# First q projection in four passes of 128 tokens, with wq's rows loaded ahead of x tiles 2 and 3

## Chip, cores and metric

One core of a Trainium2 chip runs the whole program. The metric is the device time of that core in microseconds, the median of several executions. The span in a profile, from the first to the last instruction, is about 1.8 us shorter (1616.3 us in an execution of 1618.12 us). No run here was in the slower state, so no run is left out.

## The reference, cut to what matters

```python
x = x + A(layernorm(x), wqkv, wo)      # dilated local attention, 32 heads of 32, window 8, dilation 2
x = x + B(layernorm(x), w1, w3, w2)    # SwiGLU, 1024 -> 3584 -> 1024
x = x + A(layernorm(x), wqkv, wo)
x = x + B(layernorm(x), w1, w3, w2)
# x: 1 x 2048 x 1024 bf16; wqkv: 1024 x 3072
```

The kernel works in chunks of 512 tokens, each of four tiles of 128. q, k and v are projections on TensorE. Attention itself (products, softmax, weighted sum) is elementwise work on VectorE and gives `oT`, which TensorE multiplies by `wo`.

## The kernel before

The change touches the head, which is the q projection of the first chunk. Its loads are issued in this order on the SP queue:

```python
load_tile(0, 0, 512, nc.sync)          # x tile 0, halves on two queues
load_tile(0, 512, D, nc.scalar)
load_tile(1, 0, D, nc.sync)            # every further piece here is 256 KB
loads(0, 2)                            # rows 0, 1 of wq, one DMA each
load_tile(2, 0, D, nc.sync)
loads(2, 4)
load_tile(3, 0, D, nc.sync)
loads(4, 8)                            # then k's two weight tiles (1 MB each) and x of chunk 1 (1 MB)
```

It computes q in three passes: tile 0 row by row as wq lands, tile 1 block by block, then tiles 2 and 3 together in matmuls of 256 columns. The last pass ends in four stores to DRAM, and between these stores come the loads that are needed next:

```python
for i, acc in enumerate(accumulators(2, 2 * P)):
    for b in range(2):
        for kk in range(KT):
            product(acc[:, b, :], kk, 2 * i + b, tok, kk == 0, kk == KT - 1)
    nc.scalar.copy(hT[:, 2 * i:2 * i + 2, tok], acc[:])
    nc.sync.dma_start(q_rows[:, 2 * i:2 * i + 2, 0:CH], hT[:, 2 * i:2 * i + 2, :])
    then[i]()     # x of chunk 2 | v weights | v weights | x of chunk 3
...
first_q(w_tiles[0:2], load_wq, (lambda: load_x(2), load_weight, load_weight, lambda: load_x(3)))
```

The SP queue works in order: a load written behind a store is issued only when that store's data is ready (in the kernel before, SP waits 10.6 us for the data of the first q store, and x of chunk 2 goes out behind it).

Of the kernel before, what the change touches and what calls it, by code (L numbers as in the profile page):

```python
# [7 lines left out]
FP32 = mybir.dt.float32  # L8
BF16 = mybir.dt.bfloat16
# [6 lines left out]
def kernel(  # L16
# [13 lines left out]
    nc = tc.nc  # L30
    cfg = dict(cfg or {})
    P = 128
    _, S, D = A_x.shape
    F = B_w1.shape[1]
    KT = D // P
    W, DIL, Dh = 8, 2, 32
    assert D == 1024 and KT == 8 and D // Dh == 32
    CH = 512
    NCH = S // CH
    TPC = CH // P  # L40
# [7 lines left out]
    scale = float(Dh) ** -0.5  # L48
    EPS = 1e-5
    BOOST = 3000  # L50
    NWARM = 13
    fsplits = [(0, 16), (16, NF)] if NF > 16 else [(0, NF)]
    HTN = max(b - a for a, b in fsplits)

# [21 lines left out]
    psum = ctx.enter_context(tc.tile_pool(name="psum", bufs=8, space=PSUM))  # L76
# [70 lines left out]
    ident = const.tile([P, P], BF16, name="ident")  # L147
# [13 lines left out]
    hT = const.tile([P, HTN, CH], BF16, name="hT")  # L161
# [3 lines left out]
    def warm(n):  # L165
        for i in range(n):
            pw = bank("pw")
            nc.tensor.matmul(pw[:], lhsT=zero[:, 0, 0:P], rhs=zero[:, 0:2, :].rearrange("p a b -> p (a b)"),
                             start=True, stop=True)
# [8 lines left out]
    KH = KT // 2  # L178
# [51 lines left out]
    def first_q(ws, loads, then):  # L230


        xnT = xnTs["Q", 0, 0] = xtp.tile([P, KT, CH], BF16, name="xnT")
        st = small.tile([P, TPC, 2, 6], FP32, name="st1", bufs=1)
        mv = small.tile([P, TPC, 2], FP32, name="mv1", bufs=1)
        sd = small.tile([P, TPC], FP32, name="sd1", bufs=1)
        rstd = small.tile([P, TPC], FP32, name="rstd1", bufs=1)
        q_rows = qkv_d[0][0][:].rearrange("i t s -> (i t) s").rearrange("(b p) s -> p b s", p=P)

        def load_tile(j, h0, h1, queue):  # L240
            queue.dma_start(x_sb[:, j, h0:h1], xin[:, j, h0:h1])  # L241

        load_tile(0, 0, 512, nc.sync)
        load_tile(0, 512, D, nc.scalar)
        load_tile(1, 0, D, nc.sync)
        loads(0, 2)
        load_tile(2, 0, D, nc.sync)
        loads(2, 4)
        load_tile(3, 0, D, nc.sync)
        loads(4, 8)  # L250
        preload = small.tile([P, 1], FP32, name="preload", bufs=1)
        nc.scalar.activation(preload[:], epst[:], ACTF.Sqrt)

        def stats(j, hh):
            nc.vector.bn_stats(st[:, j, hh, :], x_sb[:, j, hh * 512:(hh + 1) * 512])  # L255

        def deviation(j):
            nc.vector.bn_aggr(mv[:, j, :], st[:, j, :, :])
            nc.scalar.activation(sd[:, j:j + 1], mv[:, j, 1:2], ACTF.Sqrt, bias=epst[:])  # L259

        def apply(j, parts=1):
            nc.vector.reciprocal(rstd[:, j:j + 1], sd[:, j:j + 1])
            xn = xnp.tile([P, D], BF16, name="xn")
            for i in range(parts):
                d = slice(i * D // parts, (i + 1) * D // parts)
                nc.vector.tensor_scalar(xn[:, d], x_sb[:, j, d], mv[:, j, 0:1], rstd[:, j:j + 1],  # L266
                                        op0=ALU.subtract, op1=ALU.mult)
            return xn

        def transpose(xn):  # L270
            pTs = []
            for h in range(2):
                pT = psum.tile([P, KH, P], BF16, name="pT", tag="mm")
                for kk in range(KH):
                    nc.tensor.transpose(pT[:, kk, :], xn[:, (h * KH + kk) * P:(h * KH + kk + 1) * P], ident[:])  # L275
                pTs.append(pT)
            return pTs

        def evacuate(j, h, pTs, copy):
            copy(xnT[:, h * KH:(h + 1) * KH, j * P:(j + 1) * P], pTs[h][:])  # L280

        def product(out, kk, b, tok, start, stop):
            nc.tensor.matmul(out, lhsT=ws[kk // KH][:, kk % KH, b * P:(b + 1) * P], rhs=xnT[:, kk, tok],  # L283
                             start=start, stop=stop, skip_group_check=True)

        def accumulators(per, n):
            return [psum.tile([P, per, n], FP32, name="pq", tag="mm") for _ in range(KT // per)]

        warm(NWARM)
        stats(0, 0)  # L290
        stats(0, 1)
        deviation(0)
        stats(1, 0)
        xn = apply(0, 2)
        pTs = transpose(xn)
        evacuate(0, 0, pTs, nc.scalar.copy)
        stats(1, 1)
        evacuate(0, 1, pTs, nc.vector.tensor_copy)
        deviation(1)

        accs = accumulators(4, P)
        tok = slice(0, P)

        def step0(kk):
            for b in range(KT):
                product(accs[b // 4][:, b % 4, :], kk, b, tok, kk == 0 and b % 4 == 0, kk == KT - 1)

        for kk in range(6):
            step0(kk)
        stats(2, 0)  # L310
        xn = apply(1)
        pTs = transpose(xn)
        for h in range(2):
            evacuate(1, h, pTs, nc.scalar.copy)
        for kk in range(6, KT):
            step0(kk)
        stats(2, 1)
        deviation(2)
        for i in range(2):
            nc.scalar.copy(hT[:, 4 * i:4 * i + 4, tok], accs[i][:])  # L320

        accs = accumulators(4, P)
        tok = slice(P, 2 * P)

        def block1(b):
            for kk in range(KT):
                product(accs[b // 4][:, b % 4, :], kk, b, tok, kk == 0, kk == KT - 1)
            if b % 4 == 3:
                nc.scalar.copy(hT[:, b - 3:b + 1, tok], accs[b // 4][:])

        stats(3, 0)
        xn = apply(2)
        stats(3, 1)
        deviation(3)
        for b in range(3):
            block1(b)
        pTs = transpose(xn)
        for h in range(2):
            evacuate(2, h, pTs, nc.scalar.copy)
        xn = apply(3)  # L340
        for b in range(3, 5):
            block1(b)
        pTs = transpose(xn)
        evacuate(3, 0, pTs, nc.scalar.copy)
        evacuate(3, 1, pTs, nc.vector.tensor_copy)
        for b in range(5, KT):
            block1(b)

        tok = slice(2 * P, CH)
        for i, acc in enumerate(accumulators(2, 2 * P)):  # L350
            for b in range(2):
                for kk in range(KT):
                    product(acc[:, b, :], kk, 2 * i + b, tok, kk == 0, kk == KT - 1)
            nc.scalar.copy(hT[:, 2 * i:2 * i + 2, tok], acc[:])
            nc.sync.dma_start(q_rows[:, 2 * i:2 * i + 2, 0:CH], hT[:, 2 * i:2 * i + 2, :])
            then[i]()
        qkv_at[0, 0, 0] = now["act"] + DMA / 2

    def tree(n, mul, dst):
# [144 lines left out]
    w_tiles, due, used = [], [], [0]  # L504

    def load_weight(pieces=1):

        if len(w_tiles) == len(seq):
            return
        kind, i, n, *rest = seq[len(w_tiles)]  # L510
        if kind == "qkv":
            w = wp.tile([P, KH, D], BF16, name="wqkv", tag="w")
            step = KH // pieces
            for k0 in range(0, KH, step):
                nc.sync.dma_start(w[:, k0:k0 + step, :],
                                  wqkv_v[:, n * KH + k0:n * KH + k0 + step, i * D:(i + 1) * D])
        elif kind == "w2":
            w = wp.tile([P, 8, 512], BF16, name="w2t", tag="w")
            nc.sync.dma_start(w[:, 0:n, :], w2_v[:, i:i + n, rest[0] * 512:(rest[0] + 1) * 512])
        else:  # L520
            w = wp.tile([P, KT, FG * P], BF16, name=kind + "t", tag="w")
            v = w1_v if kind == "w1" else w3_v
            nc.sync.dma_start(w[:, :, 0:n * P], v[:, :, i * P:(i + n) * P])
        w_tiles.append(w)
# [151 lines left out]
    def load_x(c):  # L676
        nc.sync.dma_start(x_sb[:, c * TPC:(c + 1) * TPC, :], xin[:, c * TPC:(c + 1) * TPC, :])
# [3 lines left out]
    def load_wq(k0, k1):  # L681
        for kk in range(k0, k1):
            nc.sync.dma_start(w_tiles[kk // KH][:, kk % KH, :], wqkv_v[:, kk, 0:D])  # L683
        if k1 == KT:
            load_weight()
            load_weight()
            load_x(1)

    first_q(w_tiles[0:2], load_wq, (lambda: load_x(2), load_weight, load_weight, lambda: load_x(3)))
    xnT_at["Q", 0, 0], norm_left["Q", 0, 0] = now["pe"], 0  # L690
    queue_norm(("Q", 0, 1), 1, 0)
    queue_norm(("Q", 0, 1), 1, 1)
# [3 lines left out]
    for c in range(NCH):  # L696
        for which in range(3):
# [4 lines left out]
            then = ()  # L702
            if c == 0 and which == 0:
                continue
            if c == 2 and which == 0:
                then = (None, None, lambda: nc.sync.dma_start(wo[:], wo_v))
            if c == 2 and which == 1:
                then = (load_weight, None, load_weight)
# [50 lines left out]
```

## Time and profile before

| | before |
|---|---|
| median, 6 runs | 1618.99 us (1618.64 to 1619.38) |
| span of the profile | 1616.3 us |
| first k-projection matmul | 24.64 us |
| attention begins on VectorE | 47.74 us |
| last piece of `oT` of the second half chunk written | 160.67 us |

The page of the kernel before: its span, and the chain that ended last by engine, as shares of the span.

```profile
span 1616.3 us, 19263 instructions
...
PE 99%; DMA 0%; SPq 0%; DVE 0%; ACT 0%; issue 0%
```

Followed back from the last instruction, the chain stays on TensorE almost to the start. The waits of TensorE (line, what it waited for, total us, times, longest us):

```profile
PE pw L168 <- DVE psm L163: 1.2, 1, 1.2
PE pq L283 <- DVE st L255: 0.7, 1, 0.7
PE pq L283 <- ACT xnT L280: 0.4, 1, 0.4
PE pT L275 <- DVE xn L266: 0.3, 1, 0.3
```

All four are in the first 16 us. The timeline of TensorE (start us, duration us, engine, line, operation, output from inputs, count, and in brackets the idle time ahead of the group and what ended it):

```profile
10.25 1.30 PE L283 MATMUL pq<-xnT,wqkv 128*128 128x128 bf16 x16 [0.70 <-DVE st L255]
...
15.86 0.62 PE L275 MATMUL pT<-ident,xn 128*128 128x128 bf16 x8 [0.29 <-DVE xn L266]
...
24.64 114.12 PE L591 MATMUL ps<-xnT,wqkv 128*128 128x512 bf16 x528
...
159.32 3.62 PE L552 MATMUL po<-wo,oT 128*128 128x512 bf16 x16
162.78 3.62 PE L591 MATMUL ps<-xnT,wqkv 128*128 128x512 bf16 x16
```

L283 is the q projection, L591 the k and v projections, L552 the output projection by `wo`. A matmul shown alone has 0.39 us, but in a row they start every 0.216 us, so the time of a group is read from one start to the next. TensorE is full from 24.64 us on. The line at 159.32 us reads `oT` of the second half chunk. The timeline of VectorE has the first attention product and the last piece of that `oT`:

```profile
47.74 1.21 DVE L424 TENSOR_TENSOR pr<-qT,kT 128x2048 bf16<-128x2048 bf16 x1
...
160.38 0.29 DVE L371 TENSOR_TENSOR oT<-tm 128x256 bf16<-128x256 bf16 x1
```

The last piece is done at 160.38 + 0.29 = 160.67 us. The matmul that reads it is the eighth of its group, and would start at 159.32 + 7 x 0.216 = 160.83 us. **So TensorE shows no wait there, but it missed one by only 0.16 us.**

The timeline of the SP queue (issue times; "x2" is two issues merged). L355 is a q store, L677 x of chunk 2, L515 v's weights, L217 the DMA transposes and L600 the stores of k:

```profile
20.21 0.37 SPq L355 DMA_DIRECT2D qkv_d<-hT  x1
20.63 0.47 SPq L677 DMA_DIRECT2D x_sb<-in_A_x_dram  x1
21.96 0.37 SPq L355 DMA_DIRECT2D qkv_d<-hT  x1
22.37 1.12 SPq L515 DMA_DIRECT2D wqkv<-in_A_wqkv_dram  x1
...
26.94 10.12 SPq L217 DMA_TRANSPOSE xnT<-xn  x2
37.16 1.04 SPq L600 DMA_DIRECT2D qkv_d<-sgt  x2
```

### The profile page before, as it was taken

The page shows a single profiled execution, that of the slowest core. Times are in us where ns is not written, and L with a number is a line of the kernel's source. Part 1 is how long each engine was busy: PE and PEld are TensorE (multiplying, and loading weights), DVE is VectorE, ACT ScalarE, POOL GpSimd, SP SyncE. Part 2 cuts the span into 40 slices and gives each one's busy share as a digit, 9 for nine tenths or more (in the row PEclk, how much of TensorE's full clock was granted, in tenths as well). Part 3 has the DMA queues.
Part 4 walks back from the last instruction along what each step waited for, and adds up shares of the span by engine and source line. Part 5 has one row for each costly group of instructions (what it writes and reads, how often), then busy time and mean ns, then how long its engine had stood idle before and what let it go on. Part 6 is the DMA issues. An engine that isn't in the chain of part 4 may idle for free.

```text
span 1616.3 us, 19263 instructions
## 1 busy us (share of the span) xinstructions
PE 1610.7 (100%) x7609; PEld 805.3 (50%) x7609; DVE 1176.6 (73%) x1965; ACT 353.6 (22%) x547; POOL 1.9 (0%) x12
## 2 busy tenths in 40 slices
PE   9999999999999999999999999999999999999999
PEld 6666544444445544455444554445544444444444
DVE  5999898989899899998998449983599832222212
ACT  4433311212112230222302123021230212011110
POOL 0000000000000000000000000000000000000000
PEclk9999999999999999999999999999999999999999
DMA  9565855466537773577553776528684266436440
GB/s 314 149 190 158 254 178 169 129 193 190 170 105 236 222 203 125 169 208 249 160 186 120 211 239 175 186 97 259 210 223 158 93 194 170 143 108 218 157 130 27
DMA packets 336427, 285.82 MB, mean 177 GB/s; under 512 B 69712, under 2 KB 318928, under 8 KB 336208
## 3 DMA queue, kind: packets, MB, share of 16 engines
q1 hardware_dynamic: 336192, 284.46, 58.0%
q8 instruction: 59, 0.97, 0.2%
q14 instruction: 32, 0.26, 0.0%
q10 hardware_dynamic: 144, 0.13, 0.0%
HBM read 239.47 MB, written 29.36 MB: 166 GB/s over the span
## 4 chain that ended last, share of the span: by engine, by line
PE 99%; DMA 0%; SPq 0%; DVE 0%; ACT 0%; issue 0%
PE acc L658 24%; PE pu L642 24%; PE pg L634 24%; PE ps L591 20%; PE po L552 7%; PE pq L283 1%; DMA wqkv<-in_A_wqkv_dram 0%; SPq L683 0%; SPq L241 0%; DVE xn L266 0%; ACT xnT L280 0%; PE pT L275 0%; DVE st L255 0%; ACT sd L259 0%; DVE x_sb L668 0%
## 5 line engine op out<-in xcount | busy, mean ns | idle before, releaser
L642 PE MATMUL pu<-xnT,w3t 128*128 128x512 bf16 x1792 | 423.4, 379 | 0.0
L634 PE MATMUL pg<-xnT,w1t 128*128 128x512 bf16 x1792 | 423.4, 379 | 0.0
L658 PE MATMUL acc<-w2t,hT 128*128 128x512 bf16 (+1 forms) x1804 | 389.7, 378 | 0.0
L591 PE MATMUL ps<-xnT,wqkv 128*128 128x512 bf16 x1472 | 319.2, 379 | 0.0
L638 ACT ACTIVATE sg<-pg 128x512 bf16<-128x512 f32 x224 | 133.6, 597 | 773.0 <-PE pg L634 719.4
L646 DVE TENSOR_TENSOR hT<-sg,pu 128x512 bf16<-128x512 bf16 x224 | 152.6, 681 | 186.8 <-PE pu L642 177.8
L658 PEld LDWEIGHTS <-hT 128*128 128x128 bf16 x1804 | 176.5, 98 | 210.5
L642 PEld LDWEIGHTS <-w3t 128*128 128x128 bf16 x1792 | 175.4, 98 | 211.4
L634 PEld LDWEIGHTS <-w1t 128*128 128x128 bf16 x1792 | 175.3, 98 | 211.4
L591 PEld LDWEIGHTS <-wqkv 128*128 128x128 bf16 x1472 | 211.1, 143 | 106.7
L424 DVE TENSOR_TENSOR pr<-qT,kT 128x2048 bf16<-128x2048 bf16 x128 | 156.2, 1221 | 87.2 <-DMA kT<-qkv_d 85.1
L668 DVE TENSOR_TENSOR x_sb<-x_sb,acc 128x512 bf16<-128x512 bf16 x129 | 87.3, 677 | 107.6 <-PE acc L658 107.4
L484 DVE TENSOR_TENSOR tm<-At,vT 128x2048 bf16<-128x2048 bf16 x128 | 156.1, 1220 | 2.4
L595 ACT CAST sgt<-ps 128x512 bf16<-128x512 f32 x184 | 106.7, 585 | 230.7 <-PE ps L591 211.9
L369 DVE TENSOR_TENSOR tm<-tm 128x1024 bf16<-128x1024 bf16 (+1 forms) x256 | 134.5, 550 | 0.4
L369 DVE TENSOR_TENSOR pr<-pr 128x1024 bf16<-128x1024 bf16 (+1 forms) x256 | 134.0, 551 | 0.5
L552 PE MATMUL po<-wo,oT 128*128 128x512 bf16 x512 | 115.7, 379 | 0.0
L552 PEld LDWEIGHTS <-oT 128*128 128x128 bf16 x512 | 50.1, 98 | 60.1 <-DVE oT L371 0.2
L189 DVE BATCH_NORM_STATS2 st<-x_sb 128x6 f32<-128x512 bf16 x120 | 75.9, 671 | 4.6 <-DMA x_sb<-in_A_x_dram 4.6
L557 DVE TENSOR_TENSOR x_sb<-x_sb,po 128x512 bf16<-128x512 bf16 x64 | 43.3, 684 | 19.2 <-PE po L552 18.9
L638 ACT ACT_TABLE_LOAD x31 | 39.8, 1283 | 51.2 <-PE pg L634 51.0
L446 DVE STREAM_TRANSPOSE psmT<-psm 128x2048 bf16<-128x2048 bf16 x16 | 36.9, 2306 | 0.2
(85 smaller groups left out, 402.3 us busy)
## 6 DMA issues: line engine op xcount, KB each, us to landing
w1t<-in_B_w_dram SPq DMA_DIRECT2D x56, 1024.0 KB, 5.5
w3t<-in_B_w_dram SPq DMA_DIRECT2D x56, 1024.0 KB, 8.0
w2t<-in_B_w_dram SPq DMA_DIRECT2D x48, 1024.0 KB, 5.4
wqkv<-in_A_wqkv_dram SPq DMA_DIRECT2D x28, 1024.0 KB, 6.8
qkv_d<-sgt SPq DMA_DIRECT2D x92, 256.0 KB, 2.9
qT<-qkv_d SPq DMA_DIRECT2D x16, 512.0 KB, 8.4
w2t<-in_B_w_dram SPq DMA_DIRECT2D x16, 512.0 KB, 5.2
kT<-qkv_d SPq DMA_DIRECT2D x14, 544.0 KB, 9.5
```

Source lines behind the costliest of these rows:

```text
L369: nc.vector.tensor_tensor(b[:, 0:m, :], b[:, 0:m, :], b[:, m:2 * m, :], op=ALU.add)
L424: V.tensor_tensor(pr[:], qT[:], kT[:, :, k0:k0 + TCH], op=ALU.mult)
L484: V.tensor_tensor(tm[:], At[:], win, op=ALU.mult)
L552: nc.tensor.matmul(ps[:], lhsT=oT[:, t, j * P:(j + 1) * P], rhs=wo[:, t, hh * 512:(hh + 1) * 512], start=(t == 0), stop=(t == KT - 1))
L591: nc.tensor.matmul(ps[:], lhsT=ws[kk // KH][:, kk % KH, t::KT], rhs=xnT[:, kk, :], start=(kk == 0), stop=(kk == KT - 1))
L595: nc.scalar.copy(sgt[:, t - t0, :], ps[:])
L634: nc.tensor.matmul(pg[:], lhsT=w1t[:, kk, fi * P:(fi + 1) * P], rhs=xnT[:, kk, :], start=(kk == 0), stop=(kk == KT - 1))
L638: nc.scalar.activation(sg[:], pg[:], ACTF.Silu)
L642: nc.tensor.matmul(pu[:], lhsT=w3t[:, kk, fi * P:(fi + 1) * P], rhs=xnT[:, kk, :], start=(kk == 0), stop=(kk == KT - 1))
L646: nc.vector.tensor_tensor(hT[:, f - f0, :], sg[:], pu[:], op=ALU.mult)
L658: nc.tensor.matmul(acc[:], lhsT=hT[:, f - f0, j * P:(j + 1) * P], rhs=w2ts[(f - f0) // 8][:, (f - f0) % 8, q0:q0 + step], start=(f == f0), ...
L668: nc.vector.tensor_tensor(xs, xs, acc[:], op=ALU.add)
```

## The change

The intent is a shorter head. wq's rows go ahead of x tiles 2 and 3; the last pass, which needed tiles 2 and 3 together, becomes two passes of 128 tokens, so that tile 3 is needed later; the first copies out of PSUM (the memory into which TensorE writes) are cut finer, so that the first product starts sooner; and x of chunk 2 goes right behind x of chunk 1. With 128-token passes there are two q stores of 512 KB, the first at half of the last pass.

```diff
-    NWARM = 13
+    NWARM = 12
...
-        loads(0, 2)
+        loads(0, 4)
         load_tile(2, 0, D, nc.sync)
-        loads(2, 4)
+        loads(4, 8)
         load_tile(3, 0, D, nc.sync)
-        loads(4, 8)
+        load_weight()
+        load_weight()
+        load_x(1)
+        load_x(2)
...
-        pTs = transpose(xn)
-        evacuate(0, 0, pTs, nc.scalar.copy)
+        p0, p1, p2 = transpose(xn, (0, 2, 4, 8))
+        evacuate(0, p0, nc.scalar.copy)
+        evacuate(0, p1, nc.scalar.copy)
... (pass of tile 1 and 256-column pass of tiles 2 and 3 taken out)
+        for j in range(1, TPC):
+            if j + 1 < TPC:
+                xn = apply(j + 1)
+            if j + 2 < TPC:
+                for hh in range(2):
+                    stats(j + 2, hh)
+                deviation(j + 2)
+            for i, acc in enumerate(accumulators()):
+                for b in range(4):
+                    for kk in range(KT):
+                        product(j, acc[:, b, :], kk, 4 * i + b, kk == 0)
+                    if j + 1 < TPC and (i, b) == (1, 0):
+                        parts = transpose(xn, (0, 4, 8))
+                        for part in parts:
+                            evacuate(j + 1, part, nc.scalar.copy)
+                keep(j, i, acc)
+                if j == TPC - 1:
+                    nc.sync.dma_start(q_rows[:, 4 * i:4 * i + 4, 0:CH], hT[:, 4 * i:4 * i + 4, :])
+                    then[i]()
...
-    first_q(w_tiles[0:2], load_wq, (lambda: load_x(2), load_weight, load_weight, lambda: load_x(3)))
+    def load_v1():
+        load_weight()
+        load_x(3)
+
+    first_q(w_tiles[0:2], load_wq, (load_weight, load_v1))
```

More of the change, by code (lines that the diff above doesn't have):

```diff
@@ L268, in apply, with transpose, evacuate, product @@
             return xn
-        def transpose(xn):
+        def transpose(xn, cuts):
             pTs = []
-            for h in range(2):
-                pT = psum.tile([P, KH, P], BF16, name="pT", tag="mm")
-                for kk in range(KH):
-                    nc.tensor.transpose(pT[:, kk, :], xn[:, (h * KH + kk) * P:(h * KH + kk + 1) * P], ident[:])
-                pTs.append(pT)
-            return pTs
-        def evacuate(j, h, pTs, copy):
-            copy(xnT[:, h * KH:(h + 1) * KH, j * P:(j + 1) * P], pTs[h][:])
-        def product(out, kk, b, tok, start, stop):
-            nc.tensor.matmul(out, lhsT=ws[kk // KH][:, kk % KH, b * P:(b + 1) * P], rhs=xnT[:, kk, tok],
-                             start=start, stop=stop, skip_group_check=True)
-        def accumulators(per, n):
-            return [psum.tile([P, per, n], FP32, name="pq", tag="mm") for _ in range(KT // per)]
+            for k0, k1 in zip(cuts, cuts[1:]):
+                pT = psum.tile([P, k1 - k0, P], BF16, name="pT", tag="mm")
+                for kk in range(k0, k1):
+                    nc.tensor.transpose(pT[:, kk - k0, :], xn[:, kk * P:(kk + 1) * P], ident[:])
+                pTs.append((k0, k1, pT))
+            return pTs
+        def evacuate(j, part, copy):
+            k0, k1, pT = part
+            copy(xnT[:, k0:k1, j * P:(j + 1) * P], pT[:])
+        def product(j, out, kk, b, start):
+            nc.tensor.matmul(out, lhsT=ws[kk // KH][:, kk % KH, b * P:(b + 1) * P],
+                             rhs=xnT[:, kk, j * P:(j + 1) * P], start=start, stop=kk == KT - 1,
+                             skip_group_check=True)
+        def accumulators():
+            return [psum.tile([P, 4, P], FP32, name="pq", tag="mm") for _ in range(2)]
+        def keep(j, i, acc):
+            nc.scalar.copy(hT[:, 4 * i:4 * i + 4, j * P:(j + 1) * P], acc[:])
         warm(NWARM)
@@ L294, in first_q @@
         xn = apply(0, 2)
-        pTs = transpose(xn)
-        evacuate(0, 0, pTs, nc.scalar.copy)
+        p0, p1, p2 = transpose(xn, (0, 2, 4, 8))
+        evacuate(0, p0, nc.scalar.copy)
+        evacuate(0, p1, nc.scalar.copy)
         stats(1, 1)
-        evacuate(0, 1, pTs, nc.vector.tensor_copy)
+        evacuate(0, p2, nc.vector.tensor_copy)
         deviation(1)
-        accs = accumulators(4, P)
-        tok = slice(0, P)
-        def step0(kk):
-            for b in range(KT):
-                product(accs[b // 4][:, b % 4, :], kk, b, tok, kk == 0 and b % 4 == 0, kk == KT - 1)
@@ L308, in first_q @@
-        for kk in range(6):
-            step0(kk)
-        stats(2, 0)
-        xn = apply(1)
-        pTs = transpose(xn)
-        for h in range(2):
-            evacuate(1, h, pTs, nc.scalar.copy)
-        for kk in range(6, KT):
-            step0(kk)
+        xn = apply(1)
+        stats(2, 0)
         stats(2, 1)
         deviation(2)
-        for i in range(2):
-            nc.scalar.copy(hT[:, 4 * i:4 * i + 4, tok], accs[i][:])
-        accs = accumulators(4, P)
-        tok = slice(P, 2 * P)
@@ L325, in block1 @@
-        def block1(b):
-            for kk in range(KT):
-                product(accs[b // 4][:, b % 4, :], kk, b, tok, kk == 0, kk == KT - 1)
-            if b % 4 == 3:
-                nc.scalar.copy(hT[:, b - 3:b + 1, tok], accs[b // 4][:])
-        stats(3, 0)
-        xn = apply(2)
-        stats(3, 1)
-        deviation(3)
-        for b in range(3):
-            block1(b)
-        pTs = transpose(xn)
-        for h in range(2):
-            evacuate(2, h, pTs, nc.scalar.copy)
-        xn = apply(3)
@@ L341, in first_q @@
-        for b in range(3, 5):
-            block1(b)
-        pTs = transpose(xn)
-        evacuate(3, 0, pTs, nc.scalar.copy)
-        evacuate(3, 1, pTs, nc.vector.tensor_copy)
-        for b in range(5, KT):
-            block1(b)
-        tok = slice(2 * P, CH)
-        for i, acc in enumerate(accumulators(2, 2 * P)):
-            for b in range(2):
-                for kk in range(KT):
-                    product(acc[:, b, :], kk, 2 * i + b, tok, kk == 0, kk == KT - 1)
-            nc.scalar.copy(hT[:, 2 * i:2 * i + 2, tok], acc[:])
-            nc.sync.dma_start(q_rows[:, 2 * i:2 * i + 2, 0:CH], hT[:, 2 * i:2 * i + 2, :])
-            then[i]()
+        accs = accumulators()
@@ new lines, in first_q @@
+        for kk in range(KT):
+            for b in range(KT):
+                product(0, accs[b // 4][:, b % 4, :], kk, b, kk == 0 and b % 4 == 0)
+            if kk == 4:
+                parts = transpose(xn, (0, 4, 8))
+                for part in parts:
+                    evacuate(1, part, nc.scalar.copy)
+        for i in range(2):
+            keep(0, i, accs[i])
+        for j in range(1, TPC):
[7 more added lines that the diff above has]
+                for b in range(4):
+                    for kk in range(KT):
+                        product(j, acc[:, b, :], kk, 4 * i + b, kk == 0)
+                    if j + 1 < TPC and (i, b) == (1, 0):
+                        parts = transpose(xn, (0, 4, 8))
+                        for part in parts:
+                            evacuate(j + 1, part, nc.scalar.copy)
[3 more added lines that the diff above has]
+                    then[i]()
@@ L683, in load_wq @@
             nc.sync.dma_start(w_tiles[kk // KH][:, kk % KH, :], wqkv_v[:, kk, 0:D])
-        if k1 == KT:
-            load_weight()
-            load_weight()
-            load_x(1)
-    first_q(w_tiles[0:2], load_wq, (lambda: load_x(2), load_weight, load_weight, lambda: load_x(3)))
+    def load_v1():
+        load_weight()
+        load_x(3)
+    first_q(w_tiles[0:2], load_wq, (load_weight, load_v1))
     xnT_at["Q", 0, 0], norm_left["Q", 0, 0] = now["pe"], 0
```

## The prediction

> **What bounds it now.** The span is 1616.3 us; TensorE is busy 1610.7 us. The list of TensorE's waits has four entries, 2.6 us in all, all in the first 16 us. In the timeline TensorE then runs gap-free from the first k-projection matmul at 24.64 us to its end, 0.216 us per 512-column matmul. So a change of the first q projection is worth exactly how far it moves that 24.64 us.
>
> The head has two limits. (1) Until about 12.2 us it is the arrival of wq's rows: weight loads wait for a DMA before row 3 (8.92 us), row 4 (10.24) and row 5 (10.92). In the table by stretches the DMA engines are full from 7 to 18 us, near 400 GB/s. Each 256 KB piece takes 0.66 us (row 3 to row 4: two pieces, 1.32 us). (2) Then TensorE's own work, with one hole: about 0.46 us before 15.86 us, where the transposes of x tile 3 wait for its normalised rows.
>
> **What the change does.**
> - Loads. The Trainium skill ("DMA: Bandwidth & Descriptors", Queues, rings and completion order) says that an engine consumes descriptors in ring order; the trace's even spacing agrees. Before, row 7 is piece 12 (x0, x1, two rows, x2, two rows, x3, four rows); after, piece 11. Counting from row 3's 8.92 us at 0.66 us each, I estimate rows 0 to 3 at 6.3, 6.9, 7.6, 8.3; x2 8.9; rows 4 to 7 at 9.6, 10.2, 10.9, 11.56; x3 12.2 us. Before, row 7's loads start near 12.24 (40 matmuls begin at 11.78). Gain 0.68 us.
> - The hole before tile 3's transposes: they now come a whole pass later (about 18 us), x3 lands at 12.2, and ScalarE's deviation no longer stands behind it. Gain 0.46 us.
> - 64 matmuls of 256 columns (16.32 to 24.64 us less 24 small ones: 6.95 us, 0.109 each) become 128 of 128 columns at 0.0557 (40 matmuls, 11.83 to 14.06): 7.13 us. Cost 0.18 us. The skill's isolated gap of N/2.4 + 2.5 ns ("TensorE: Matmul & The Clock Gate", Back-to-back issue gap) says 56 and 109 ns, as measured.
> - One warm-up matmul less and the earlier first product (about 7.0 instead of 7.35 us): nothing, since row 7 ends pass 0 in either case.
> - k's weights and x of chunk 1 keep their place; x of chunk 2 fills the DMA dip at 18 to 22 us. q stores become two of 512 KB. No stall for TensorE.
>
> **Sum.** Row 7 at 11.56, its 8 matmuls to 12.0, 192 matmuls at 0.0557 = 10.7, two groups of transposes at 0.45: the k projection starts at 23.6 us instead of 24.64. Everything after moves along unchanged. Gain 1.0 us of 1618.9: predicted 1617.9 us, range 1616.8 to 1619.1. Faster by over 2%: 0.005; within 2%: 0.99; slower: 0.005.
>
> **What would show it.** First k matmul near 23.6 us; row 7's weights near 11.6; weight loads waiting for DMA before most rows of pass 0; no wait between 12 and 24 us; TensorE without gaps later; matmul time of passes 1 to 3 about 3.6 us each.
>
> **What would make it wrong.** ScalarE is tight: tile 1's copies out of PSUM stand behind tile 2's deviation, which waits for x2; they end near 11.9, so a late x2 stalls pass 1. Rows may land later than even spacing says. TensorE waits for rows through pass 0, and if its clock dropped there, 128-column passes would show it. A new gap at the k or v weights would also take back the gain. Run-to-run spread (0.7 us before) is nearly as large as the effect.

## More of the kernel before

```python
# normalised x of later chunks is transposed by DMA, issued from the same SP queue
nc.sync.dma_start_transpose(out=xnT[:, :, j * P:(j + 1) * P], in_=xn[:])
...
# k and v: ScalarE copies the product into one of 3 staging buffers, SP stores it (stg: bufs=3)
nc.scalar.copy(sgt[:, t - t0, :], ps[:])
...
# output projection: TensorE needs oT, which VectorE's attention makes
for t in range(KT):
    nc.tensor.matmul(ps[:], lhsT=oT[:, t, j * P:(j + 1) * P], rhs=wo[:, t, hh * 512:(hh + 1) * 512], ...)
```

The order of each engine's instructions is fixed when the program is built. A projection by `wo` is placed at a point of TensorE's order, and if `oT` isn't there by then, TensorE stands.

## The result, and the profile after

| | before | after |
|---|---|---|
| median, 6 runs each | 1618.99 us | 1619.0 us (1618.81 to 1619.2) |
| span of the profile | 1616.3 us | 1617.2 us |
| first k-projection matmul | 24.64 us | 23.99 us |
| attention begins | 47.74 us | 48.75 us |
| last piece of that `oT` written | 160.67 us | 161.69 us |

The ratio is 1.000 (95% interval 0.9987 to 1.0013). A ratio is the mean time of one kernel's fast runs over that of the other's of the same rounds, so it is not quite the ratio of the medians quoted here. The time did not move, yet the head did become shorter: k starts 0.65 us sooner. The profile shows where that went. The page of the changed kernel:

```profile
span 1617.2 us, 19240 instructions
...
PE 89%; DVE 8%; issue 1%; DMA 1%; ACT 1%; SPq 0%; ACTq 0%; DVEq 0%
```

The chain that ended last no longer stays on TensorE: 8% of it is on VectorE. TensorE's waits in the changed kernel:

```profile
PE po L539 <- DVE oT L358: 1.2, 2, 0.9
PE pw L168 <- DVE psm L163: 1.2, 1, 1.2
PE pq L287 <- DMA wqkv<-in_A_wqkv_dram: 0.5, 1, 0.5
PE pT L278 <- DVE xn L269: 0.3, 1, 0.3
```

There is a new one, `po` (the output projection) waiting for `oT`. In TensorE's timeline (L287 q, L578 k and v, L539 output projection):

```profile
9.89 0.62 PE L287 MATMUL pq<-xnT,wqkv 128*128 128x128 bf16 x8 [0.45 <-DMA wqkv<-in_A_wqkv_dram]
...
23.99 114.13 PE L578 MATMUL ps<-xnT,wqkv 128*128 128x512 bf16 x517
...
158.68 1.46 PE L539 MATMUL po<-wo,oT 128*128 128x512 bf16 x6
161.08 0.39 PE L539 MATMUL po<-wo,oT 128*128 128x512 bf16 x1 [0.95 <-DVE oT L358]
161.75 2.12 PE L539 MATMUL po<-wo,oT 128*128 128x512 bf16 x9 [0.27 <-DVE oT L358]
163.70 3.62 PE L578 MATMUL ps<-xnT,wqkv 128*128 128x512 bf16 x15
```

Up to 158.68 us TensorE is ahead of the kernel before by 0.64 us (158.68 against 159.32). Undisturbed, the 16 matmuls of the group take 3.45 us (159.32 to 162.78). Here 163.70 - 158.68 = 5.02 us pass, a stall of 1.57 us. From there on it is 163.70 against 162.78, that is 0.92 us behind, and it stays so: the spans differ by 0.9 us. So the head gave 0.65 us and one stall took 1.57.

(The spans of the two profiles differ by 0.9 us, but the medians by nothing. One profile is one execution, and k's start scatters from run to run by some 0.4 us, as the table of runs further down shows. In its second profile the unchanged head, in e2_before_v_early, started k at 25.01 us instead of 24.64. That is not the whole 0.9 us: the six timed executions of the kernel before have spans of about 1616.8 to 1617.6, their times less 1.8, and none is as quick as the profiled one.)

VectorE explains the stall. The first attention product and the last piece of that `oT`:

```profile
48.75 1.21 DVE L411 TENSOR_TENSOR pr<-qT,kT 128x2048 bf16<-128x2048 bf16 x1
...
161.40 0.29 DVE L358 TENSOR_TENSOR oT<-tm 128x256 bf16<-128x256 bf16 x1
```

Attention begins 1.01 us later than before, and its `oT` is done 1.02 us later. What holds VectorE until 48.75 us is seen in the chain of waits of the changed kernel between 22 and 50 us (start us, us, what):

```profile
38.19 2.47 DMA qkv_d<-sgt
...
40.76 0.06 ACT sgt L582
...
41.62 0.20 ACT sd L194
...
48.83 1.14 DVE pr L411
```

From the end backwards: VectorE's statistics go in step with ScalarE's square roots (`sd`). ScalarE had to wait before 40.76 us with the copy of k into a staging buffer (`sgt`), because the store that was to free this buffer (`qkv_d<-sgt`) was issued only at 38.19 us. It stood idle for 5.05 us there; in the kernel before for 3.48 us, until 39.76. That store stood on the SP queue behind the two DMA transposes (L217). The SP queue:

```profile
23.01 0.37 SPq L342 DMA_DIRECT2D qkv_d<-hT  x1
23.43 0.51 SPq L502 DMA_DIRECT2D wqkv<-in_A_wqkv_dram  x1
...
27.22 10.87 SPq L217 DMA_TRANSPOSE xnT<-xn  x2
38.19 1.05 SPq L587 DMA_DIRECT2D qkv_d<-sgt  x2
```

L342 is the first q store, L502 v's first weights, L217 the transposes and L587 the stores of k. v's weights were issued at 23.43 and 25.21 us, before at 22.37 and 24.40. x of chunk 3 behind them went out at the same time as before (25.88 and 25.86 us). The stores of k were issued at 38.19 instead of 37.16 us, about the 1.01 us that attention lost. Of these 1.03 us only 0.28 lie in the start of the transposes (27.22 against 26.94); the other 0.75 is that the two transposes held the queue for 10.87 instead of 10.12 us. In the second profile of the changed kernel, e7_after_again, they started at 26.93 us, as before, and held it for 11.68. The table by stretches from 22 to 24 us (columns: busy us of TensorE, its weight loads, VectorE, ScalarE, GpSimd, each with instructions, then the granted TensorE clock, DMA share, GB/s), the kernel before and then the changed one:

```profile
22.00:24.00 2.00, 2.00 (x21) 1.78 (x20) 1.97 (x5) 0.58 (x1) 0.00 (x0) 1.00 0.96 196
...
22.00:24.00 2.00, 2.00 (x40) 2.00 (x38) 1.94 (x4) 0.58 (x1) 0.00 (x0) 1.00 0.18 67
```

In the changed kernel the DMA engines move 67 GB/s there: x of chunk 2 had been loaded early, and nothing else had been let go. (Before, a like gap lay at about 19 to 21 us.)

### The profile page after: what moved, and what is told of

Its sections match the earlier page's. It is cut to its first block, busy times and chain, and to the rows that moved or that the text cites. A ratio compares the mean times of both kernels' runs of the same rounds, so it can differ in the third digit from the quotient of the medians.

```text
span 1617.2 us, 19240 instructions
## 1 busy us (share of the span) xinstructions
PE 1603.3 (99%) x7525; PEld 806.0 (50%) x7672; DVE 1176.4 (73%) x1964; ACT 354.0 (22%) x549; POOL 1.9 (0%) x12
## 4 chain that ended last, share of the span: by engine, by line
PE 89%; DVE 8%; issue 1%; DMA 1%; ACT 1%; SPq 0%; ACTq 0%; DVEq 0%
PE acc L645 24%; PE pg L621 23%; PE pu L629 23%; PE ps L578 12%; PE po L539 6%; DVE pr L411 1%; DVE tm L471 1%; DVE tm L356 1%; DVE pr L356 1%; DVE st L189 1%; PE pq L287 1%; DMA wqkv<-in_A_wqkv_dram 1%; DVE xn L214 0%; DVE At L455 0%; DVE L L435 0%
## 5 line engine op out<-in xcount | busy, mean ns | idle before, releaser
L578 PE MATMUL ps<-xnT,wqkv 128*128 128x512 bf16 x1440 | 317.5, 379 | 1.7
L578 PEld LDWEIGHTS <-wqkv 128*128 128x128 bf16 x1472 | 211.1, 143 | 106.8
L539 PE MATMUL po<-wo,oT 128*128 128x512 bf16 x503 | 115.4, 379 | 1.8 <-DVE oT L358 1.2
L539 PEld LDWEIGHTS <-oT 128*128 128x128 bf16 x512 | 50.0, 98 | 61.7 <-DVE oT L358 2.0
```

The lines of the kernel that those rows point to most:

```text
L578: nc.tensor.matmul(ps[:], lhsT=ws[kk // KH][:, kk % KH, t::KT], rhs=xnT[:, kk, :], start=(kk == 0), stop=(kk == KT - 1))
```

## The experiments

The theory (A): the head's gain is real. It is lost because v's weights and x of chunk 3 are let go only by q stores, and these now come later. So the DMA transposes end later on the queue, the stores of k and then attention come late, and TensorE meets an unfinished `oT`. Rivals: B, the chain on VectorE is set by something else than these loads; C, x of chunk 2 going ahead delays the rest; D, early loads are worth something by themselves. Each experiment is compared with the kernel before on the same chip. All were correct.

The table holds what the argument rests on, in us. "k" is the first k matmul and "att" the first attention product. "late" is the end of the last piece of `oT` less the moment at which TensorE would read it, which is k + 136.19, from before's 160.83 - 24.64. "stall" is what TensorE's timeline shows at that group over 3.45 us.

| run | k | att | late | stall | span | median | before, same chip |
|---|---|---|---|---|---|---|---|
| before | 24.64 | 47.74 | -0.16 | 0 | 1616.3 | 1618.99 | |
| after | 23.99 | 48.75 | 1.51 | 1.57 | 1617.2 | 1619.0 | 1618.99 |
| e1_v_early | 23.76 | 46.04 | -1.01 | 0 | 1615.4 | 1617.11 | 1618.83 |
| e2_before_v_early | 25.01 | 46.27 | -1.76 | 0 | 1616.7 | 1618.01 | 1618.83 |
| e3_dve_1us | 24.83 | 48.61 | 0.48 | 0.56 | 1617.1 | 1619.07 | 1618.83 |
| e4_x2_back | 23.67 | 50.62 | 3.65 | 5.27 | 1620.6 | 1622.59 | 1618.83 |
| e5_rows_only | 23.96 | 47.72 | 0.48 | 0.55 | 1616.2 | 1618.18 | 1618.52 |
| e6_wide_last | 23.74 | 46.73 | -0.27 | 0 | 1615.4 | 1617.04 | 1618.52 |
| e7_after_again | 24.04 | 49.25 | 1.93 | 1.99 | 1617.7 | 1619.23 | 1618.52 |
| e8_early_dve_1us | 23.93 | 47.75 | 0.55 | 0.62 | 1616.2 | 1617.99 | 1618.52 |
| e9_quarter_stores | 23.37 | 47.45 | 0.79 | 0.86 | 1615.9 | 1617.9 | 1618.85 |
| e10_rows_first | 23.87 | 45.83 | -1.31 | 0 | 1615.5 | 1616.71 | 1618.85 |
| e11_v_early_again | 23.92 | 46.11 | -1.11 | 0 | 1615.6 | 1617.37 | 1618.85 |

Two regularities hold in every row. The last piece of `oT` ends 112.9 us after attention begins (112.89 to 112.94; 113.17 in e2_before_v_early, where VectorE also had to wait 0.18 us for TensorE). And the span is k + 1591.66 us (1616.3 - 24.64, from before) + stall, within 0.1 us.

### e1_v_early

```diff
         load_x(2)
+        load_weight()
+        load_weight()
+        load_x(3)
...
-                    then[i]()
```

> The changed kernel with v's two weight tiles and x of chunk 3 issued ahead of the q stores, right behind x of chunk 2. Theory A (the 0.65 us won in the head is lost because the attention chain on VectorE starts 1.01 us late, 48.75 instead of 47.74 us, since v's weights wait on the queue behind the later and larger q stores; TensorE then stalls 1.5 us on oT near 159 us): attention starts well before 47.7 us (estimate 43 to 46), the stall on oT is gone, the k projection still starts at about 24.0 us, and the span is 1.5 us under the changed kernel's 1617.2, that is near 1615.65; time ratio to before 0.9996. Rival B (the chain on VectorE is set by other things than these loads, and always ends about 160.6 us): the stall on oT stays at 0.8 to 1.5 us and the span stays at 1616.3 to 1617.2.

Measured: attention at 46.04 us, no wait for `oT`, span 1615.4, median 1617.11 against 1618.83 (ratio 0.999, interval 0.9976 to 1.0003). TensorE's timeline:

```profile
158.45 3.62 PE L541 MATMUL po<-wo,oT 128*128 128x512 bf16 x16
161.90 3.62 PE L580 MATMUL ps<-xnT,wqkv 128*128 128x512 bf16 x16
```

The group at 158.45 takes its 3.45 us. Expected was a span near 1615.65, so theory A holds and rival B falls. Attention began somewhat later than my 43 to 46. The interval includes 1, but the lists are plain: the five runs (1616.92 to 1617.91) all lie below the nine of before (1617.92 to 1619.19), if only just.

### e2_before_v_early

```diff
# the kernel before
             load_x(1)
+            load_x(2)
+            load_weight()
+            load_weight()
+            load_x(3)
...
-            then[i]()
```

> The kernel before, with the same early loads (x of chunk 2, v's weights, x of chunk 3 ahead of the q stores) and nothing else. Theory A: attention starts earlier here too, so its last piece of oT is ready seconds tenths or microseconds before TensorE asks for it at 159.32, but TensorE had no stall there to lose, so the span stays at 1616.3 within 0.3 us and the ratio is 1.000. Rival B: same start of attention, same span. Rival D (early loads are worth something by themselves): span down by 0.5 us or more.

Measured: attention 1.5 us sooner (46.27), span 1616.7, ratio 0.9995 (0.9983 to 1.0008). Its k started at 25.01 us in the profile, and 25.01 + 1591.66 is the span: no stall, and nothing won from the early attention. The median is 0.8 us under before's; the lists overlap (1617.67 to 1618.51). So rival D isn't shown by the profile and not excluded by the times: by the medians, early loads alone give about half of e1_v_early's 1.7 us. The two profiles are a poor pair for this. e2's was taken of its slowest execution of five (1618.51), before's of a quick one (1618.12). By the second regularity, k plus stall is 24.5 us in e2's median execution (a span of 1616.2) and 25.3 in before's on this chip (1617.0). An estimate from these: the usual execution of the kernel before already waits some tenths of a microsecond for `oT`, and early loads take that wait away. No profile shows it.

### e3_dve_1us

```diff
# the kernel before: a memset whose result is overwritten, as attention begins
-            yield 0.0, ready, lambda: None
+            yield 0.0, ready, (lambda: V.memset(psm[:], 0.0)) if g == 0 else (lambda: None)
```

> The kernel before, with one idle memset of about 1.0 us on VectorE as attention begins, loads and head untouched. Before, the last piece of oT ends at 160.67 us and the matmul that reads it would start at 159.32 + 7 x 0.216 = 160.83 us: 0.16 us of slack. Theory A: the k projection still starts at 24.6 us, TensorE stalls near 159 us, and the span grows by 1.0 - 0.16 = about 0.85 us to 1617.15; ratio 1.0005. If the slack is larger than it seems (the stall has another cause): span unchanged.

Measured: the memset took 0.91 us, attention began at 48.61 (0.87 later than before's), and TensorE stalled 0.56 us at the same group as in the changed kernel. With k at 24.83, which is 0.19 later than in before's profile, the slack was 0.35 us, and 0.87 - 0.35 = 0.52. Span 1617.1 as expected, though in part from the late k; the median rose by only 0.24 us (ratio 1.0002). The mechanism is shown by itself: loads and head untouched, VectorE alone made late, and TensorE stands at `oT`. In its timeline the group is split where it waits:

```profile
159.50 1.78 PE L552 MATMUL po<-wo,oT 128*128 128x512 bf16 x7
161.56 2.12 PE L552 MATMUL po<-wo,oT 128*128 128x512 bf16 x9 [0.27 <-DVE oT L371]
```

### e4_x2_back

```diff
# the changed kernel
         load_x(1)
-        load_x(2)
...
+    def load_x2_v0():
+        load_x(2)
+        load_weight()
...
-    first_q(w_tiles[0:2], load_wq, (load_weight, load_v1))
+    first_q(w_tiles[0:2], load_wq, (load_x2_v0, load_v1))
```

> The changed kernel with x of chunk 2 back in its old place behind the first q store, so that v's weights stand one further 1 MB load (2.6 us at the measured rate) down the queue. Theory A: attention starts up to 2.6 us later still, about 50 to 51.3 us, the stall on oT grows from 1.5 us to 2.7 to 4.1 us and the span to 1618.4 to 1619.8. Rival C (it is x of chunk 2 going ahead that delays the queue): attention goes back to about 47.7 us, the stall falls to 0.5 us and the span to 1616.2.

Measured: attention at 50.62, ratio 1.0024 (1.0011 to 1.0036): slower by a quarter of a per cent, clear of the noise. Rival C falls: x of chunk 2 ahead is the part of the change that helps. The start of attention is as expected, but the stall of 5.27 us is larger than the 2.7 to 4.1 expected. TensorE's timeline and then the table by stretches (us, busy us of each engine with instructions, granted TensorE clock, DMA share, GB/s):

```profile
160.51 0.39 PE L538 MATMUL po<-wo,oT 128*128 128x512 bf16 x1 [0.90 <-DVE oT L357]
162.91 0.39 PE L538 MATMUL po<-wo,oT 128*128 128x512 bf16 x1 [2.01 <-DVE oT L357]
163.57 3.68 PE L538 MATMUL po<-wo,oT 128*128 128x512 bf16 x9 [0.27 <-DVE oT L357]
167.09 3.62 PE L577 MATMUL ps<-xnT,wqkv 128*128 128x512 bf16 x16
```

```profile
164.00:165.00 1.00, 1.00 (x4) 0.42 (x3) 0.97 (x2) 0.00 (x0) 0.00 (x0) 0.50 0.39 78
165.00:166.00 1.00, 1.00 (x4) 0.30 (x2) 0.97 (x2) 0.00 (x0) 0.00 (x0) 0.50 0.88 193
...
167.00:168.00 1.00, 1.00 (x7) 0.64 (x6) 0.71 (x2) 0.00 (x0) 0.00 (x0) 1.00 1.09 383
```

Waits of 0.90, 2.01 and 0.27 us stand in the group. The granted clock is still 1.00 up to 163.2 us, 0.50 from 163.4, when the third wait had just begun, also 0.50 in the stretches from 164 to 166 us, and 1.00 again from 167. The nine matmuls from 163.57 to 167.09 took 3.52 us, where at 0.216 us each they take 1.94: 1.58 us of the stall are clock, and the remaining 3.69 are the lateness of 3.65. The Trainium skill ("TensorE: Matmul & The Clock Gate", Part 1) says that an idle array falls to half its clock after an idle window of about 3.4 us. This run agrees on the half, but its longest single wait was 2.01 us. In the changed kernel, with waits of 0.95 and 0.27 us, the clock stayed at 1.00.

### e5_rows_only

```diff
# the kernel before
-        loads(0, 2)
+        loads(0, 4)
         load_tile(2, 0, D, nc.sync)
-        loads(2, 4)
+        loads(4, 8)
         load_tile(3, 0, D, nc.sync)
-        loads(4, 8)
... (k's weights and x of chunk 1 follow as before)
```

> The kernel before with the new order of the row loads alone (four rows, x tile 2, four rows, x tile 3); its three passes and everything else stay. Additive theory (the terms of the prediction add up): row 7 lands one piece sooner, so the k projection starts 0.68 us sooner than in the unchanged kernel's profiles (24.6 to 25.0), about 24.1. Theory H (in the old passes the head is held by x tile 3, since its statistics stand ahead of tile 2's and tile 3's normalisation on VectorE): x tile 3 lands at 12.3 to 12.6 as before, tile 3's transposes stay at about 15.9 to 16.2, the gap before them grows from 0.3 to about 0.9 us, and the k projection starts at 24.6 to 25.0; time unchanged, ratio 1.000.

Measured: k at 23.96 us, the gap before tile 3's transposes still 0.31 us, span 1616.2, ratio 0.9999. My theory H was wrong and the sum of terms right: x tile 3 is not what holds the old passes, and the row order alone gives 0.68 us (before's 24.64) or more (0.87 against the mean of the three old heads). But attention stayed at 47.72, so TensorE arrived early at `oT` and stalled 0.55 us. TensorE's timeline:

```profile
158.64 1.77 PE L554 MATMUL po<-wo,oT 128*128 128x512 bf16 x7
160.69 2.12 PE L554 MATMUL po<-wo,oT 128*128 128x512 bf16 x9 [0.27 <-DVE oT L373]
```

This is the cleanest sight of the limit: the head gets shorter, attention starts no later than before, and most of the gain is still gone. (Here the stores of k were issued at 36.46 us, 0.70 sooner than before, and attention was still not earlier: ScalarE waited 2.85 us for a later store, until 46.82 us. So the first store of k is not the only one that can hold attention.)

### e6_wide_last

```diff
# e1_v_early, with tiles 2 and 3 again in one pass (tile 3's transposes moved into pass 1)
+        for i in range(4):
+            acc = psum.tile([P, 2, 2 * P], FP32, name="pq", tag="mm")
...
+                    nc.tensor.matmul(acc[:, b, :], ..., rhs=xnT[:, kk, tok], ...)
```

> Early loads as in e1_v_early, and the last two passes of 128 tokens made one of 256 again, with tile 3's transposes moved up into pass 1. The 256-column matmuls cost 0.109 us each against two of 0.0557: the k projection starts 0.18 us sooner than in e1_v_early (23.76), about 23.6, and the span is 0.2 us under 1615.4. If tile 3's copies out of PSUM come late for the wide pass, a gap of 0.1 to 0.3 us takes it back.

Measured: k at 23.74, span 1615.4, ratio 0.9991: as e1_v_early. From tile 2's transposes to k it took 23.74 - 14.50 = 9.24 us against 23.76 - 14.38 = 9.38, so 0.14 of the 0.18 us are there, but rows landed 0.12 us later in this run. Two passes or one are the same within what one profile can tell.

### e7_after_again

```diff
(none: the changed kernel)
```

> The changed kernel once more, for a second profile. In its first profile x tile 0 was ready at 4.09 us, in every other profile so far at 3.60 to 3.69. If that is scatter: x tile 0 at 3.6 to 3.7, row 7's weights at 11.6 to 11.7, k projection at 23.6 to 23.8; attention starts again at 48 to 49 us, so the stall on oT is 1.5 to 2 us and the span is again 1616.8 to 1617.3: what the head gains, the stall takes. If the late x is caused by the row loads queued behind it: 4.1 us again and the k projection at 24.0.

Measured: x tile 0 at 3.68 us, so the 4.09 of the first profile was scatter. But k started at 24.04 all the same, since row 4 landed late (its product started at 9.94). Attention at 49.25, stall 1.99, span 1617.7, above what I expected; ratio 1.0005. The stall is the rule for this kernel and not an accident of one profile.

### e8_early_dve_1us

```diff
# e1_v_early, with the memset of e3_dve_1us
```

> e1_v_early with the same idle 0.9 us memset on VectorE that cost the kernel before about 0.5 us. With early loads the last piece of oT ended at 158.94 us and was wanted at 158.45 + 7 x 0.216 = 159.96: 1.0 us of slack. Theory A: no stall, or under 0.1 us, span as e1_v_early, 1615.4 within 0.3. If the memset costs for another reason than the slack: 0.5 to 0.9 us more.

Measured: a stall of 0.62 us, span 1616.2, ratio 0.9998. The expectation failed. Attention began 1.71 us later than in e1_v_early, of which the memset is only 0.9. Most of the other 0.8 us is in the loads: the stores of k were issued at 35.24 instead of 34.60 us. With 112.9 us from there the lateness is 0.55, which the stall fits. So the rule holds, but the slack of e1_v_early is not a safe 1.0 us; it is some tenths when the DMA queue has a slow run.

### e9_quarter_stores

```diff
# the changed kernel: last pass in four quarters, a q store behind each
+        for i in range(4):
+            acc = psum.tile([P, 2, P], FP32, name="pq", tag="mm")
...
+            nc.sync.dma_start(q_rows[:, 2 * i:2 * i + 2, 0:CH], hT[:, 2 * i:2 * i + 2, :])
+            then[i]()
...
-    first_q(w_tiles[0:2], load_wq, (load_weight, load_v1))
+    first_q(w_tiles[0:2], load_wq, (load_weight, load_weight, lambda: None, lambda: load_x(3)))
```

> The changed kernel with the last pass's accumulators in four quarters and a q store behind each, v's weights behind the first and second store, x of chunk 3 behind the last: only the moment at which v's loads are let go is moved, from 23.4 to about 21.3 us. So far, in every run, the last piece of oT ended 112.9 us after attention began, and TensorE wanted it 136.2 us after the first k matmul; the stall was the difference. Theory A: the hole in the DMA rate at 22.3 to 24 us closes, attention starts 1 to 2 us before the changed kernel's 48.75 and 49.25, about 47 to 48; with the k projection at 23.7 to 24.0 (wanted: attention no later than 46.9 to 47.2) the stall falls from 1.6 to 2.0 to 0.2 to 1.0 us, span 1615.6 to 1616.6. If the moment of v's loads is not the cause: attention at 48.7 to 49.3, stall 1.5 us or more, span near 1617.4.

Measured: v's first weights issued at 21.70 us, attention at 47.45 (1.3 and 1.8 us sooner than the changed kernel's two profiles), stall 0.86, span 1615.9, ratio 0.9995 (0.9982 to 1.0007). The moment at which v's loads are let go was moved, and attention and stall moved with it. But the edit makes the q stores smaller at the same time (256 KB instead of 512), and k itself started early, at 23.37 us, since the rows landed early. So the run says that the coarse q stores of the change did the harm; whether by their time or by their size it can't say. In e1_v_early the loads don't wait for any q store, the stores keep their 512 KB, and the stall is gone, which speaks for the time.

### e10_rows_first and e11_v_early_again

```diff
# e10_rows_first, from e1_v_early
-        loads(0, 4)
-        load_tile(2, 0, D, nc.sync)
-        loads(4, 8)
+        loads(0, 8)
+        load_tile(2, 0, D, nc.sync)
         load_tile(3, 0, D, nc.sync)
+        load_x(1)
         load_weight()
         load_weight()
-        load_x(1)
... (tile 2's statistics behind tile 1's copies, transposes one block later)
```

> An attempt at a better version, from e1_v_early: all eight rows of wq ahead of x tiles 2 and 3, x of chunk 1 ahead of k's weights, tile 2's statistics and its transposes put where their data then is. Row 7 lands one piece (0.66 us) sooner, so the k projection starts at about 23.1 to 23.3 us instead of 23.76; attention, whose statistics of chunk 1 need not wait for k's weights, starts before 46 us, and no stall on oT follows. Span 1614.7 to 1615.0. If tile 2 is late instead, a gap before its transposes or before pass 2 shows and the gain shrinks.

> e1_v_early once more, for comparison on the same chip: attention at 45.9 to 46.9, no stall on oT, k projection at 23.7 to 24.0, span 1615.3 to 1615.8.

Measured: e10_rows_first has the best median, 1616.71 against 1618.85 of before (ratio 0.9987, interval 0.9975 to 1.0; 1616.56 to 1617.33 against 1618.48 to 1619.13). Its profile doesn't show the expected head: tile 2 was indeed late, with a gap before its transposes at 14.87 us, and k started at 23.87. But that profile is of the slowest of the five executions (1617.33). The other four have spans of 1614.8 to 1615.0, as expected, and by the second regularity k at about 23.1 to 23.3. e11_v_early_again repeats e1_v_early: 1617.37, all five runs below all nine of before. So the 0.66 us between the two medians is not seen in their profiles (spans 1615.5 and 1615.6); which part of the head won it was not profiled.

## Why the prediction was right or wrong

The time lay in the range. The predicted point, 1617.9, was 1.1 us too low, and the gain of 1.0 us did not appear.

- **The head: right.** k was predicted at 23.6 us. The six profiles of this head (after, e1, e4, e7, e8, e11) have 23.67 to 24.04, mean 23.88; the three of the old head (before, e2, e3) have 24.64 to 25.01, mean 24.83. The gain is 0.95 us against the predicted 1.0. Both absolute values were 0.2 to 0.3 us off, since one profile of before was taken for its usual state and rows landed some tenths later than even spacing says (row 4's product at 9.88 against 9.6, row 7's weights at 11.92 against 11.56).
- **The terms of the head.** Row 7 sooner: e5_rows_only has it alone, 0.68 to 0.87 us. The hole before tile 3: gone. The 128-column passes: 0.14 of the predicted cost of 0.18 us in e6_wide_last. Small terms of the right size.
- **"So a change of the first q projection is worth exactly how far it moves that 24.64 us": this step failed,** and with it "Everything after moves along unchanged" and "No stall for TensorE". TensorE without gaps after 24.64 us meant that nobody was later than it, not that nobody was close. VectorE was: in the stretch from 48 to 150 us it was busy 98.6 of 102 us, and it delivered `oT` 0.16 us ahead of need in the profile of before. A second chain, of its own length (112.9 us from the start of attention), ran beside TensorE and met it at 160 us. Shortening one of two such chains gives no more than the slack.
- **"q stores become two of 512 KB" was seen, but not what hangs on them.** v's weights and x of chunk 3 are let go by these stores. v's weights went out 1.06 and 0.81 us later, the DMA transposes held the queue 0.75 us longer, and through the stores of k and ScalarE's staging buffers attention moved 1.01 us back. The prediction read the early x of chunk 2 as filling a dip; the dip only moved.
- That the time lay in the range was luck: the range allowed for scatter, not for this. The small slack and the later attention, neither of them foreseen, together undid the gain almost exactly.

What stays open: why the transposes held the queue longer, and so why attention was late by 1.0 to 1.5 us. Between 24 and 30 us the changed kernel moved 274, 236 and 291 GB/s in the three stretches of 2 us, where before moved 326, 401 and 401. Whether the larger stores, or what stands beside them, slow the flow was not tried by itself. The medians of e2_before_v_early and e10_rows_first are 0.5 and 0.6 us under their profiled executions, which were the slowest of five; what their usual execution looks like was not profiled, and neither was that of the kernel before.

## What to carry to other kernels

Before saying that a gain on the busiest engine carries through, look up at every later meeting point how early the other engine's data was ready there: no wait in the list can mean 0.16 us of slack. Loads written behind a store on an in-order queue are let go by that store; when the store is moved, follow what stands behind it to the engine that needs it. In the changed kernel a head made 0.95 us shorter was worth nothing until the loads of the second chain were let go early as well, and then both together gave 1.5 to 2.1 us by the medians. The early loads alone, with the old head, gave 0.8 us by the medians, with lists that overlap. Where gains are this small, look at which execution a profile shows before setting it against another.

## What the Trainium skill lacked or had wrong

- "TensorE: Matmul & The Clock Gate", Back-to-back issue gap: it gives about 81 ns for N = 128 and 131 ns for N = 512 in a stream of weight load and matmul pairs. Here such streams ran at 55.7 ns (40 matmuls of 128 columns from 11.83 to 14.06 us) and 216 ns (16 of 512 columns from 159.32 to 162.78 us). Its formula for the isolated gap, 56 and 216 ns, is what the streams kept.
- The same page, Why this matters for your kernels: the advice is no idle gap over about 3 us. In e4_x2_back the clock fell to 0.50 with a longest gap of 2.01 us: two gaps, 0.90 and 2.01 us, with one matmul between them, and a third just begun, were enough. In e7_after_again gaps of 1.36 and 0.27 us left it at 1.00.
- "Perfetto Trace Analysis", DMA Instruction — HWDGE: it says that the reported time of an issue includes waiting for the descriptor generator, but not how long that can hold a queue. In the kernel before, the issue of one DMA transpose held SP for 6.05 us and the next for 3.96, in a stretch (26 to 37 us) in which the DMA share was 1.06 to 1.13; the median of its 60 such issues is 1.29 us. In the changed kernel the same two held it for 10.87 us together, and the stores of k stood behind them.
- The same page, Identifying the Most-Contended Engine: it ranks engines by occupancy. Over the whole span that gives TensorE 100% and VectorE 73%; from 48 to 150 us VectorE was at 97% and met TensorE within 0.16 us, and even there the ranking names TensorE. No page speaks of slack at a meeting point of two engines.
